# A fused retention and gated-MLP kernel whose engine order is a table: one table exchanged for another

## The chip, the cores and the metric

The kernel runs on one core of a Trainium2 chip. The metric is device time in microseconds (us), the median of three runs. One execution was also profiled by the hardware.

## The reference

A retention layer (a linear attention with a decaying state) feeds a gated MLP with a spatial gate. Everything is float32; B = 4, H = 8, S = 768, D = 64, model width 512.

```python
for t in range(S):                                   # retention, for each batch and head
    state = gamma * state + k[t] (x) v[t]
    y[t] = scale * q[t] @ state
x = y.transpose(0, 2, 1, 3).reshape(B, S, H * D)
h = gelu_tanh(x @ w_in)                              # moe: [B, S, 1024]
u, v = h[..., :512], h[..., 512:]
v_n = (v - mean(v)) / sqrt(var(v) + 1e-6) * g_ln
v_s = einsum('ts,bsd->btd', w_sg, v_n) + b_sg[None, :, None]
out = x + (u * v_s) @ w_out
```

## The kernel before

The work is cut into four batches b and two half sequences h of 384 positions; a pair of heads is p = 0..3. Each piece is a small function, and a table of words, `PROG`, calls them one after the other. A word is a letter and its indices, with D, G or A behind it where the piece may run on VectorE (DVE), GpSimd (POOL) or ScalarE (ACT): `I012D` is piece I of batch 0, half 1, pair 2, on VectorE. The schedule is manual: each engine works through its words in the order of the table and waits only for data and for buffers. So the table is the order of every engine and of the DMA issues of SyncE (SP).

The words that the change and the prediction speak of:

- L loads a pair's keys and values; `lo2`, `ls5` and the like load raw weights (of w_out and w_sg). All of these go through SP.
- P scales the keys (ACT or POOL), S and D are the score and state matmuls (TensorE, PE; tiles sc and ds), M masks the scores and T scans the states (DVE), W lays the scanned states beside the scores (ACT or POOL), O is the retention output (PE, tile po), X scales it into x (DVE), H and I split x into two float32r parts (cast and difference, tile xh).
- V and U are the two halves of the first MLP matmul (PE, tiles pv and pu), v and u their gelus (ACT), s the statistics (DVE), N the reciprocal deviation (six small operations of POOL, lines 378 to 383), n the normalisation (DVE, line 388), a and b its split (tile vh).
- G is the spatial matmul (PE, tile ps), e its scale and offset (DVE, line 435), m the gate, h and j the split of the product (tile gh), Y the last matmul (PE, tile py), r the residual and y the store.
- weights: r, k, c, b, a turn raw 64-bit words into float32, `hs7` and `os7` split part 7 of w_sg (lines 149 or 151, and 224).

All matmuls of the MLP are made of three float32r passes. PSUM has four banks for the retention (S, D and O share them) and four for the MLP, so a matmul that opens a bank waits for the reader of an earlier one: `S102` for `X100`, which reads `O100`, and `Y1000` for `e103`, which reads the last of four G banks.

Of the kernel before, what the change touches and what calls it, by code (L numbers as in the profile page):

```python
# [48 lines left out]
W0100A O003 bv1 ls2 W0101A av1 X003 H003A O010 lu3 I003D hv1A ls11 X010 U0001 hs0A ov1D ku2 H010A os0G V0011
ku1 L012 V0001 cu2 P011A cu1 V0012 ru2 bu2 ls9 ro3 V0002 bu1 ls1 ru1 V0013 I010G u000 V0003 v001 au2 V0021  # L50
s001 ru3 v000 S011 au1 hu2A s000 D011 ku3 M011 ou2G V0022 ko3 L013 hu1A T011 V0023 P012A ou1D S012 W0111A cu3
D012 co3 W0110A bu3 U0010 L100 v002 bo3 s002 au3 U0020 lo1 M012 lo0 U0011 P013A N00 ls7 hu3A T012 lo2 U0021
u001 W0120A ou3G O011 u002 S013 W0121A n000 n001 D013 a000 n002 O012 a001 b000D L101 ro1 b001D U0030 P100A
# [5 lines left out]
U0131 u012 n011 n012 O100 u013 n010 ho0G D102 a010 X100 a011 ao1 O101 T102 H100A D103 I100G a012 S102 ho1A
S103 b012D ho2A L110 X101 b010G W1021A G0020 M103 C111 L111 G0000 H101G M102 C110 b011G V1020 G0001 I101D oo0D  # L60
V1021 oo1G G0021 P110A oo2G G0002 ho3G G0022 e000 K102 m000D G0010 P111A oo3G h000 G0030 r000D G0011 j000G
G0031 W1020G T103 G0012 W1030A K103 G0032 W1031G e001 e002 V1010 m001G G0100 m002D h001 r001G h002 V1011 G0101
j002D j001D e003 r002G O102 D110 m003D O103 X102 h003 r003G T110 H102A D111 I102G S110 W1101A S111 j003D L112
M110 W1100G V1022 Y0000 T111 L113 C112 M111 G0102 W1110A W1111G C113 X103 Y0001 e010 H103G m010D G0110 I103D
y000 r010G P112A V1023 G0111 v102 s102 Y0020 G0120 P113A Y0021 G0121 y002 G0112 V1012 e011 Y0010 m011G V1013
r011D U1000 v101 s101 G0122 U1001 V1000 u100 Y0011 V1001 y001 G0130 V1002 G0131 V1003 G0132 v100 s100 Y0030
N10 U1010 h010 h011 Y0031 j010D n102 U1011 n100 n101 a100 j011D O110 a101 e012 b100G u101 D112 e013 a102 O111
X110 b101G T112 H110A D113 S112 y003 W1121A m013G S113 M112 L200 W1120G U1020 M113 m012G L201 Y0110 T113 h012
U1030 h013 j012G U1021 b102D I110D Y0100 j013D u102 X111 W1131G P200A V1100 r012D Y0111 H111G r013D U1031
I111G y011 V1120 W1130G P201A u103 V1101 V1121 Y0101 U1100 y010 V1110 O112 D200 X112 O113 H112A T200 D201  # L70
I112G S200 K200 X113 S201 W2001G M200 L202 H113A W2000G V1102 M201 V1122 I113G L203 V1111 T201 V1103 W2010A
W2011G V1123 v110 K201 V1112 v112 s110 Y0130 s112 P202A V1113 Y0131 v111 s111 Y0120 y013 N11 P203A U1110 Y0121
n110 n112 a110 U1111 n111 y012 b110G a111 U1120 a112 u111 b111D U1101 b112D U1121 u110 G1020 u112 G1000 G1021
U1130 G1022 G1030 U1131 G1031 u113 G1010 G1032 G1011 G1001 G1012 G1002 O200 e100 e101 D202 m100G X200 O201
H200A T202 m101G D203 h100 W2020A j100D S202 r100D h101 S203 e102 I200G L210 W2021A M202 G1100 r101G L211 X201
C210 G1120 K202 M203 H201A C211 G1101 m102D j101D h102 V2010 T203 r102G G1102 e103 W2031A j102G Y1000 W2030A
m103D e110 P210G G1121 h103 j103D Y1020 I201D r103D m110G Y1001 P211G Y1021 y100 K203 r110G Y1010 y102 V2011
Y1011 V2000 y101 G1122 V2001 V2020 O202 D210 X202 O203 H202A T210 D211 I202G S210 W2101A W2100G S211 X203 L212
M210 H203G V2012 C213 I203G M211 V2021 C212 L213 V2002 T211 V2013 W2111A V2022 W2110A V2003 V2023 v201 v200
s201 U2000 v202 s200 P212A U2010 s202 U2001 N20 U2011 u200 P213G Y1030 u201 n202 G1110 n201 h110 n200 j110G  # L80
Y1031 G1111 y103 G1130 G1112 a200 a201 b200D G1131 e111 b201G e112 U2020 a202 m112D U2030 m111G G1132 b202D
h111 h112 r111D U2031 j112G U2021 j111G e113 u203 m113G O210 u202 D212 r112G X210 h113 O211 H210A T212 j113G
D213 S212 W2121A I210D S213 W2120A r113D L300 M212 Y1130 T213 L301 Y1120 M213 W2130A W2131G Y1131 X211 Y1121
H211G y113 I211G V2100 y112 P300A Y1110 V2101 Y1111 V2120 P301A y111 V2110 V2121 V2111 Y1100 O212 D300 X212
O213 H212A T300 D301 I212G W3001A S300 K300 X213 W3000A S301 M300 L302 H213G V2122 I213G M301 V2102 L303 V2123
T301 V2103 v212 W3011G Y1101 W3010A s212 K301 v210 U2100 y110 s210 P302A U2110 V2112 U2111 V2113 P303A U2101
u211 v211 U2120 s211 u210 N21 U2130 U2121 n211 U2131 n210 u212 n212 a210 a211 O300 b210D a212 D302 b211G u213
X300 O301 H300A T302 b212G D303 W3021A S302 I300D S303 W3020G M302 L310 V3000 K302 X301 C310 G2030 L311 T303
H301A C311 G2010 I301D W3030A M303 K303 W3031G G2031 G2000 P310A G2032 G2001 G2011 P311A G2002 G2012 e200
m200G V3010 e201 V3001 m201D h200 r200G V3011 h201 G2020 j200D j201G O302 r201D D310 X302 O303 T310 H302A D311  # L90
I302G S310 W3101A W3100G S311 X303 L312 M310 H303A G2021 C313 I303G T311 C312 L313 V3012 M311 W3110A W3111G
G2022 V3013 e202 V3002 e203 m202G v301 Y2020 s301 m203G h202 Y2030 j202G h203 Y2000 j203D r202G Y2021 P313A
r203D Y2031 y202 P312G Y2001 y203 Y2010 y200 G2100 Y2011 G2120 y201 G2101 G2110 G2121 G2111 G2122 G2112 G2102
V3003 e210 e211 O310 v300 m210D D312 s300 m211G h210 O311 X310 r210G D313 h211 T312 S312 H310G W3121A S313
j210D I310D V3020 M313 W3120G G2130 r211G T313 V3021 X311 W3131A W3130G G2131 e212 H311A j211D V3022 M312
m212G G2132 I311G h212 V3023 e213 j212G Y2130 v302 r212D Y2120 s302 m213D Y2100 N30 h213 Y2110 j213D O312 n302
n300 O313 X312 r213G a300 Y2131 H312A b300D Y2101 n301 y213 I312G a301 Y2121 a302 y210 b301G X313 V3120 y212
Y2111 b302D H313G V3121 I313D y211 U3100 V3122 U3101 V3123 u310 V3100 v312 V3110 s312 V3101 V3111 V3102 V3112
V3103 V3113 v310 U3110 s310 v311 s311 U3120 N31 U3111 U3121 u311 n310 n312 U3130 a310 n311 u312 b310G a311
U3000 a312 U3131 b311D b312G U3010 u313 U3001 U3011 u300 G3000 u301 G3010 G3001 G3011 G3002 G3012 e300 m300G  # L100
U3020 e301 m301G h300 U3030 j300D h301 U3021 r300G U3031 u302 j301D r301G G3020 u303 G3030 G3021 G3031 G3022
G3032 e302 m302G e303 G3100 m303D h302 Y3020 r302D h303 j302D r303G G3101 j303D G3110 G3102 Y3021 e310 m310D
Y3030 y302 r310G G3130 G3111 G3131 G3112 G3132 e311 m311D Y3031 r311G G3120 y303 Y3010 G3121 Y3000 G3122 h310
# [482 lines left out]
```

## Time and profile before

| | |
|---|---|
| median of three runs | 410.04 us (409.76 to 411.33) |
| the profiled execution | 412.78 us, of which the span is 411.0 |
| TensorE | 398.8 us busy, 97% of the span |
| VectorE, GpSimd, ScalarE | 233.7, 180.6 and 145.4 us busy |

The span is what the profile shows, from the first instruction to the last. TensorE's busy time holds its warm-up matmuls (word `~40`, to 12 us) and matmuls that run at half clock, so it isn't all useful work.

### The profile page before, as it was taken

Reading aid. Unit: us, or ns where it says so; the run is one execution under the profiler, and the core shown is the slowest. Engines: PE = TensorE matmul, PEld = TensorE weight load, DVE = VectorE, ACT = ScalarE, POOL = GpSimd, SP = SyncE. Lnnn points to the kernel's source line nnn. Section 1 sums busy time; section 2 is a strip of 40 time slices with the busy share of each in tenths; the row PEclk is TensorE's granted clock in tenths of the full one; section 3 lists DMA queues with packets and bytes.
Section 4 is the critical chain, followed back from the end, with each engine's and each line's share of the span. In section 5 each row is a group of like instructions: output and inputs, shape, how many; then the busy total and the mean of one; then the engine's idle time right before and its main releaser. Section 6 shows DMA issues by size and latency. Waiting matters only on the chain.

```text
span 411.0 us, 9318 instructions
## 1 busy us (share of the span) xinstructions
PE 398.8 (97%) x3921; PEld 365.4 (89%) x3922; DVE 233.7 (57%) x373; ACT 145.4 (35%) x265; POOL 180.6 (44%) x217
## 2 busy tenths in 40 slices
...
GB/s 245 301 356 282 210 281 115 49 154 3 84 109 21 27 166 108 107 2 4 150 59 155 21 76 138 172 4 155 10 170 54 2 2 77 2 0 2 20 39 96
DMA packets 18122, 41.38 MB, mean 101 GB/s; under 512 B 2464, under 2 KB 8096, under 8 KB 18080
## 3 DMA queue, kind: packets, MB, share of 16 engines
...
q14 instruction: 11, 0.09, 0.1%
...
## 4 chain that ended last, share of the span: by engine, by line
PE 79%; DVE 9%; DMA 5%; issue 3%; POOL 1%; SPq 1%; ACT 1%; DVEq 0%
PE ps L425 24%; PE py L463 16%; PE pv L352 13%; PE pu L408 13%; PE po L320 5%; PE ds L271 4%; PE sc L279 4%; DMA raw<-in_w_u_dram 2%; DMA kt<-in_kk_dram 2%; DVE mw L297 2%; DVE sq L284 2%; DMA raw<-in_w_sg_dram 1%; DVE v L388 1%; DVE wx L188 1%; DVE ws L224 1%
## 5 line engine op out<-in xcount | busy, mean ns | idle before, releaser
L425 PE MATMUL ps<-ws,vh 128*128 128x384 f32 x576 | 107.8, 337 | 0.0
L425 PEld LDWEIGHTS ps<-ws,vh 128*128 128x128 f32 x576 | 101.5, 189 | 1.7
L352 PE MATMUL pv<-wv,xh 128*128 128x512 f32 x288 | 76.6, 400 | 1.4 <-ACT xh L149 1.3
L463 PE MATMUL py<-gh,wo 128*128 128x384 f32 x384 | 73.0, 336 | 1.1 <-DVE gt L435 1.1
L408 PE MATMUL pu<-xh,wu 128*128 128x384 f32 x384 | 73.0, 340 | 0.0
L463 PEld LDWEIGHTS py<-gh,wo 128*128 128x128 f32 x384 | 67.4, 188 | 2.9 <-issue 1.4
L408 PEld LDWEIGHTS pu<-xh,wu 128*128 128x128 f32 x384 | 67.4, 188 | 1.4 <-ACT v L362 0.2
L352 PEld LDWEIGHTS pv<-wv,xh 128*128 128x128 f32 x288 | 52.5, 188 | 12.4 <-ACT xh L149 2.1
L435 DVE SCALAR_TENSOR_TENSOR gt<-ps,gb 128x384 f32<-128x384 f32 x32 | 19.0, 611 | 57.9 <-PE ps L425 56.9
L446 POOL TENSOR_TENSOR gt<-gt,u 128x384 f32<-128x384 f32 x19 | 19.8, 1049 | 62.5 <-DVE gt L435 48.6
L149 ACT COPY mw<-sq 64x320 f32<-64x320 f32 (+1 forms) x41 | 33.8, 824 | 29.0 <-DVE sq L284 28.7
L297 DVE TENSOR_TENSOR mw<-sc,tab 64x384 f32<-64x384 f32 x64 | 35.5, 555 | 6.5 <-PE sc L279 4.9
L320 PEld LDWEIGHTS po<-mw 128*64 128x64 f32 (+1 forms) x768 | 26.6, 137 | 9.1 <-issue 5.0
L450 ACT CAST gh<-gt 128x384 fp32r<-128x384 f32 x32 | 16.2, 514 | 52.1 <-POOL gt L446 27.3
L320 PE MATMUL po<-mw 128*64 128x64 f32 (+1 forms) x768 | 31.6, 227 | 2.5 <-DVE sq L284 1.4
L339 POOL TENSOR_TENSOR xh<-x,xh 128x384 fp32r<-128x384 f32 x19 | 19.6, 1031 | 31.0 <-ACT xh L149 30.6
L284 DVE TENSOR_TENSOR_SCAN sq<-step,ds 128x384 f32<-128x384 f32 x32 | 30.2, 942 | 4.0 <-PE ds L271 2.1
L478 DVE TENSOR_TENSOR o<-py,o 128x384 f32<-128x384 f32 x32 | 17.6, 553 | 25.7 <-PE py L463 25.2
L366 DVE BATCH_NORM_STATS2 st<-v 128x6 f32<-128x512 f32 x24 | 16.4, 684 | 24.0 <-ACT v L362 23.9
L474 POOL TENSOR_TENSOR o<-xh 128x384 f32<-128x384 f32 x19 | 22.1, 1168 | 16.1 <-DVE gt L446 15.2
L362 ACT ACTIVATE v<-pv 128x512 f32<-128x512 f32 x24 | 14.3, 602 | 41.0 <-PE pv L352 40.9
L279 PE MATMUL sc<-mw,kt 64*64 64x64 f32 x768 | 26.9, 223 | 1.9 <-DVE x L327 1.8
...
## 6 DMA issues: line engine op xcount, KB each, us to landing
kt<-in_kk_dram SPq DMA_DIRECT2D x32, 384.0 KB, 5.2
...
```

Source lines behind the costliest of these rows:

```text
L149: nc.scalar.copy(out=out, in_=in_)
L279: mm(out=scs[u][o, c], lhsT=kt[i, c], rhs=mv[j][i, c], start=True, stop=True)
L284: nc.vector.tensor_tensor_scan(out=sqs[u].rearrange("p e c -> p (e c)"), data0=step_t[:, p].rearrange("p e c -> p (e c)"), data1=dss.pop(u ...
L297: nc.vector.tensor_tensor(out=mv[j][h], in0=sc[h], in1=mask_t[h, p : p + 1, :].to_broadcast([64, NCH, C]), op=ALU.mult,)
L320: mm(out=pos[u][o, c], lhsT=w[j][i, c], rhs=mv[j][i, c], start=True, stop=True)
L339: engines[e].tensor_tensor(out=t[:, p, 1], in0=xs.pop((b, hf, p)), in1=t[:, p, 0].bitcast(F32), op=ALU.subtract)
L352: mm(out=pv[b, hf, k], lhsT=x[:, p, a, k * 128 : (k + 1) * 128], rhs=wv_t[:, w, p], start=(p == 0 and n == 0), stop=(p == NP - 1 and n == 2),)
L408: mm(out=pu[b, hf, f], lhsT=wu_t[:, w, f, p * 128 : (p + 1) * 128], rhs=x[:, p, a], start=(n == 0), stop=(n == 11),)
L425: mm(out=ps[b, hf, d], lhsT=vh[b, t][:, v, d * 128 : (d + 1) * 128], rhs=ws_t[hf * NT + t][:, w], start=(n == 0), stop=(n == 3 * NT - 1),)
L446: engines[e].tensor_tensor(out=t, in0=t, in1=ut.pop((b, hf, d)), op=ALU.mult)
L463: mm(out=py[b, hf, c], lhsT=wo_t[c][:, w, d * 128 : (d + 1) * 128], rhs=gh[b, hf, d][:, a], start=(d == 0 and n == 0), stop=(d == 3 and n ...
L474: engines[e].tensor_tensor(out=o, in0=x[:, 0], in1=x[:, 1], op=ALU.add)
```

## The change

Only `PROG` is exchanged. The multiset of pieces is the same; 120 of the 1,224 words run on another engine, and many stand elsewhere. The counts of words on each engine stay about the same: DVE 316 before and 318 after, ACT 263 and 261, POOL 170 and 170, PE 416 and SP 89 in both. One line of the table and the line that stands at the same place after the change:

```diff
-hs9A os1D hs4A D100 os5D hs11A X013 hs2G D101 hs10A T100 H013A os9G S100 hs6A hs7A S101 I013D L102 hs8A os6D
+O013 hs1A D100 hs3G hs4A X013 D101 hs2G hs11A T100 H013A os9G S100 hs10A hs6A S101 I013D hs8A L102 os1D hs7A
```

The words of the diff are few to a reader; what follows are three places of the two orders, engine by engine.

VectorE in the first batch, from the splits of w_sg (`os`, line 224) to `X100` (line 327). Before, the rows from the last `os` over M (297), s (366 and 369), T (284), M and n (388) to X are:

```order
L224 TENSOR_TENSOR ws<-raw,ws 128x384
L297 TENSOR_TENSOR mw<-sc,tab 64x384 x2
L366 BN_STATS st<-v 128x6
L369 BN_AGGR mvar<-st 128x2
L284 SCALAR_TENSOR_TENSOR sq<-step,ds 128x384
L366 BN_STATS st<-v 128x6
L369 BN_AGGR mvar<-st 128x2
L366 BN_STATS st<-v 128x6
L369 BN_AGGR mvar<-st 128x2
L297 TENSOR_TENSOR mw<-sc,tab 64x384 x2
L388 TENSOR_SCALAR v<-v,mvar,lny 128x512 x3
L327 TENSOR_TENSOR x<-po,tab 128x384
```

and after the change:

```order
L224 TENSOR_TENSOR ws<-raw,ws 128x384 x6
L297 TENSOR_TENSOR mw<-sc,tab 64x384 x2
L366 BN_STATS st<-v 128x6
L369 BN_AGGR mvar<-st 128x2
L366 BN_STATS st<-v 128x6
L369 BN_AGGR mvar<-st 128x2
L366 BN_STATS st<-v 128x6
L369 BN_AGGR mvar<-st 128x2
L284 SCALAR_TENSOR_TENSOR sq<-step,ds 128x384
L297 TENSOR_TENSOR mw<-sc,tab 64x384 x2
L388 TENSOR_SCALAR v<-v,mvar,lny 128x512 x3
L327 TENSOR_TENSOR x<-po,tab 128x384
```

The scan `T101` moved behind the three statistics, and with it M behind it is `M100`, which both `O100` on PE needs. In front, six `os` stand in a row (`os1 os3 os6 os2 os4 os8`); before there were four there and one weight operation (`bo1`, line 188), and two others further up. POOL has `os7 os10 os11 ao1` beside them after the change, and had `os3 os2 os7` and, later, `os11` before; `ao1` stood behind N.

ScalarE in the same batch, from the split of x for pair 1 (`H011`, tile xh) to the W that `O013` needs (tile mw). Before:

```order
L149 CAST xh<-x 128x384
L394 CAST vh<-v 128x512
L178 ACTIVATE wx<-raw 128x512
L418 ACTIVATE u<-pu 128x384
L178 ACTIVATE wx<-raw 128x512
L149 CAST xh<-x 128x384
L197 ACTIVATE raw<-raw 128x512
L178 ACTIVATE wx<-raw 128x512
L256 ACTIVATE kt<-kt,tab 128x384
L149 COPY mw<-sq 64x64x6
```

and after:

```order
L149 CAST xh<-x 128x384
L197 ACTIVATE raw<-raw 128x512
L394 CAST vh<-v 128x512
L197 ACTIVATE raw<-raw 128x512
L149 CAST ws<-raw 128x384
L149 CAST xh<-x 128x384
L418 ACTIVATE u<-pu 128x384
L178 ACTIVATE wx<-raw 128x512 x2
L149 COPY mw<-sq 64x64x6
L256 ACTIVATE kt<-kt,tab 128x384
L149 COPY mw<-sq 64x64x6
```

Between the two `xh` rows (`H011` and `H012`) stood `a002 ko2 u003 ko0` (lines 394, 178, 418, 178); now `ro1 a002 ro0 hs5` (197, 394, 197 and 149, ws) stand there, and `ko2 ro2` went ahead of the first. Of the two W of `O013`, one came over from POOL. On SP, the loads of w_out come in the order `lo2 lo1 lo0` with `ls5 ls11` behind them, where it was `lo1 lo0 ls7 lo2`.

VectorE in the second batch, at the change from the G of half 0 to those of half 1. Before, from `j100` to `e103` (lines 454 and 435):

```order
L454 TENSOR_TENSOR gh<-gt,gh 128x384
L474 TENSOR_TENSOR o<-xh 128x384
L435 SCALAR_TENSOR_TENSOR gt<-ps,gb 128x384
L297 TENSOR_TENSOR mw<-sc,tab 64x384 x2
L327 TENSOR_TENSOR x<-po,tab 128x384
L297 TENSOR_TENSOR mw<-sc,tab 64x384 x2
L446 TENSOR_TENSOR gt<-gt,u 128x384
L454 TENSOR_TENSOR gh<-gt,gh 128x384
L284 SCALAR_TENSOR_TENSOR sq<-step,ds 128x384
L435 SCALAR_TENSOR_TENSOR gt<-ps,gb 128x384
```

and after:

```order
L454 TENSOR_TENSOR gh<-gt,gh 128x384
L435 SCALAR_TENSOR_TENSOR gt<-ps,gb 128x384
L297 TENSOR_TENSOR mw<-sc,tab 64x384 x2
L284 SCALAR_TENSOR_TENSOR sq<-step,ds 128x384
L297 TENSOR_TENSOR mw<-sc,tab 64x384 x2
L435 SCALAR_TENSOR_TENSOR gt<-ps,gb 128x384
```

Between `j100` and `e103` VectorE has eight pieces before and four after (an M is one piece of two instructions); `j101`, one of the eight, went to POOL. On PE, `O202 D210 O203 D211 S210 S211` now stand between the last G of half 0 and the first of half 1, and `G1100 G1120` alone between those and `Y1000`; before, `G1100 G1120 G1101 V2010 G1102` stood there.

## Rows read from the trace of the kernel before

**Rows 1.** The page's first line: the span of the profiled execution.

```profile
span 411.0 us, 9318 instructions
```

**Rows 2.** Windows: length, each engine's busy time (instructions), granted clock, DMA share, GB/s.

```profile
32.00:34.00 2.00, 1.18 (x35) 1.04 (x33) 1.23 (x2) 1.88 (x3) 1.20 (x1) 1.00 1.06 296
...
84.00:86.00 2.00, 2.00 (x48) 1.96 (x42) 1.19 (x2) 2.00 (x5) 1.12 (x2) 0.57 0.04 12
...
204.00:404.00 200.00, 200.00 (x1802) 189.73 (x1802) 100.07 (x162) 53.96 (x98) 78.21 (x96) 1.00 0.20 60
```

**Rows 3.** Timeline of TensorE: start, length, instruction, [idle before <-who ended it].

```profile
78.17 1.22 PE L320 MATMUL po<-mw 64*64 64x64 f32 x24
...
81.02 0.92 PE L271 MATMUL ds<-mw,kt 64*64 64x64 f32 x24
83.74 2.41 PE L279 MATMUL sc<-mw,kt 64*64 64x64 f32 x48 [1.81 <-DVE x L327]
86.08 3.08 PE L425 MATMUL ps<-ws,vh 128*128 128x384 f32 x12
89.00 0.85 PE L352 MATMUL pv<-wv,xh 128*128 128x512 f32 x3
```

**Rows 4.** The chain that ended last: the same matmuls elsewhere (start, length).

```profile
107.84 1.40 PE sc L279 x48
...
119.17 2.08 PE ps L425 x12
```

**Rows 5.** Timeline of VectorE, 67 to 84 us.

```profile
67.54 3.24 DVE L224 TENSOR_TENSOR ws<-raw,ws 128x384 fp32r<-128x384 f32 x3
70.71 1.50 DVE L188 SCALAR_TENSOR_TENSOR wx<-raw,wx 128x512 int32<-128x512 int32 x1
72.13 0.55 DVE L224 TENSOR_TENSOR ws<-raw,ws 128x384 fp32r<-128x384 f32 x1
...
74.58 0.93 DVE L284 TENSOR_TENSOR_SCAN sq<-step,ds 128x384 f32<-128x384 f32 x1
...
76.93 0.18 DVE L369 BATCH_NORM_AGGREGATE mvar<-st 128x2 f32<-128x6 f32 x1
77.14 1.14 DVE L297 TENSOR_TENSOR mw<-sc,tab 64x384 f32<-64x384 f32 x2
79.56 3.67 DVE L388 TENSOR_SCALAR v<-v,mvar,lny 128x512 f32<-128x512 f32 x3 [1.27 <-POOL lny L383]
83.14 0.54 DVE L327 TENSOR_TENSOR x<-po,tab 128x384 f32<-128x384 f32 x1
```

**Rows 6.** Timeline of GpSimd, 67 to 80 us.

```profile
67.75 3.91 POOL L224 TENSOR_TENSOR ws<-raw,ws 128x384 fp32r<-128x384 f32 x3
...
77.20 0.24 POOL L378 TENSOR_SCALAR lna<-mvar 128x3 f32<-128x3 f32 x1 [0.34 <-DVE mvar L369]
...
79.33 0.19 POOL L383 TENSOR_TENSOR lny<-lny,lnt 128x3 f32<-128x3 f32 x1
```

**Rows 7.** Timeline of TensorE, 56 to 64 us.

```profile
56.51 3.90 PE L352 MATMUL pv<-wv,xh 128*128 128x512 f32 x15 [0.67 <-ACT xh L149]
61.08 2.49 PE L352 MATMUL pv<-wv,xh 128*128 128x512 f32 x9 [0.67 <-ACT xh L149]
63.49 1.05 PE L320 MATMUL po<-mw 128*64 128x64 f32 x24
```

**Rows 8.** Timeline of ScalarE, 59 to 63 us.

```profile
59.02 0.67 ACT L178 ACTIVATE wx<-raw 128x512 f32<-128x512 f32 x1 [2.05 <-DMA raw<-in_w_out_dram]
...
62.69 0.89 ACT L149 COPY mw<-sq 64x384 f32<-64x384 f32 x1
```

**Rows 9.** Timelines of TensorE and VectorE near 200 us.

```profile
200.97 1.28 PE L463 MATMUL py<-gh,wo 128*128 128x384 f32 x6 [1.12 <-DVE gt L435]
...
200.24 0.58 DVE L435 SCALAR_TENSOR_TENSOR gt<-ps,gb 128x384 f32<-128x384 f32 x1
```

**Rows 10.** DMA issues of the page: size, median time from issue to landing.

```profile
kt<-in_kk_dram SPq DMA_DIRECT2D x32, 384.0 KB, 5.2
```

More of the change, by code (lines that the diff above doesn't have):

```diff
@@ L49 @@
[L49 to L53, printed above, removed]
@@ L54 @@
-X011 ao3 ro0 Q M013 V0120 ls5 H011A ls3 U0031 a002 I011D T013 b002G ko2 V0121 u003 X012 V0110 ko0 co2 V0100
-W0130G H012A ro2 V0111 I012D ko1 co0 V0101 P101A bo2 V0122 W0131A bo0 V0112 co1 hs5A ao2 V0102 hs1A hs3A O013
-hs9A os1D hs4A D100 os5D hs11A X013 hs2G D101 hs10A T100 H013A os9G S100 hs6A hs7A S101 I013D L102 hs8A os6D
-W1000A U0100 os4D os10D L103 V0123 bo1 os8D U0101 v012 M101 K100 W1001A os3G V0113 u010 s012 V0103 os2G v011
-T101 U0110 v010 os7G s011 P102A U0120 W1011A K101 s010 os11G W1010A U0111 M100 N01 U0130 u011 P103A U0121 ao0
@@ L59 @@
[L59 to L103, printed above, removed]
@@ new lines @@
+O003 bv1 ls9 W0101A ls6 av1 X003 lu3 H003A O010 I003D hv1A L012 X010 U0001 hs0A ov1D ku2 P011A os0D V0011 cu2
+ku1 V0001 H010G ls8 ru2 bu2 V0012 ls3 ru1 I010D V0002 ro3 cu1 au2 u000 V0013 V0003 v001 bu1 V0021 hu2A s001
+au1 v000 S011 ru3 s000 D011 ku3 ou2G M011 ko3 V0022 L013 P012A T011 hu1G S012 D012 ls2 ou1D W0111A cu3 V0023
+L100 W0110A co3 bu3 U0010 v002 bo3 lo2 U0020 s002 au3 lo1 lo0 M012 U0011 N00 P013A ls5 T012 hu3A ls11 U0021
+u001 W0120A ou3G O011 u002 S013 W0121A n000 D013 n001 a000 n002 O012 a001 L101 b000D P100A U0030 b001D ko2
@@ new lines @@
+X011 ao3 Q ro2 V0120 M013 ls7 H011A V0110 ro1 I011D U0031 a002 co2 ls1 X012 ro0 b002G T013 V0121 hs5A H012A
+V0111 os5D u003 V0100 ko0 I012D bo2 ko1 V0122 co0 W0130A V0101 co1 bo0 P101A V0112 bo1 W0131A V0102 ao2 hs9A
+O013 hs1A D100 hs3G hs4A X013 D101 hs2G hs11A T100 H013A os9G S100 hs10A hs6A S101 I013D hs8A L102 os1D hs7A
+U0100 W1000A os3D os6D L103 V0123 os2D os4D U0101 v012 os8D W1001A M101 K100 V0113 os7G u010 V0103 s012 v011
+os10G U0110 v010 s011 P102A os11G U0120 s010 ao1 T101 U0130 M100 W1011A U0121 N01 W1010A U0131 P103A K101 u012
@@ new lines @@
+n011 U0111 u013 n012 n010 O100 ao0 u011 a010 D102 a011 X100 b010G O101 a012 T102 H100A D103 ho0A b012D S102
+W1020A I100G S103 ho1A M102 L110 b011G ho2A G0020 ho3A X101 L111 M103 C111 G0000 H101A oo1G C110 W1021A V1020
+I101D G0001 oo2G V1021 oo0D G0002 P110A oo3G G0021 e000 K102 m000G T103 G0010 W1030A K103 G0022 r000D h000
+P111G W1031A G0011 j000G G0030 G0012 G0031 e001 e002 m001G V1010 G0032 m002D h001 r001D h002 V1011 j001D r002D
+G0100 e003 j002G Y0000 m003D r003D h003 G0101 j003D Y0001 G0102 y000 G0110 e010 m010D G0120 r010G G0111 G0121
@@ new lines @@
+X200 b112G T202 H200A D203 I200G S202 S203 W2020G X201 L210 M202 H201A G1020 K202 C210 W2021G L211 M203 C211
+G1000 I201G T203 G1021 W2031A K203 G1030 W2030A G1022 P210A G1031 G1010 G1032 P211G G1011 G1001 G1012 G1002
+O202 e100 e101 D210 m100G X202 O203 T210 m101G h100 D211 S210 W2100A j100D W2101G S211 e102 h101 L212 M210
+m102G G1100 T211 C213 L213 j101G h102 G1120 M211 W2111A j102G Y1000 W2110A e103 r100G G1101 C212 r101D Y1020
+m103G G1121 P212G h103 j103G G1102 r102G Y1001 e110 P213A r103D Y1021 m110D y100 H202G Y1010 r110G y102 V2000
@@ new lines @@
+I202D Y1011 X203 H203G V2001 I203G y101 V2010 V2020 V2011 V2021 V2012 G1122 V2013 V2022 v201 V2002 s201 V2023
+V2003 v202 Y1030 s202 v200 s200 U2000 h110 j110G U2010 N20 U2001 U2011 u200 n202 n201 Y1031 u201 n200 G1110
+y103 G1130 G1111 a200 a201 b200D G1131 b201D U2020 a202 b202G G1132 U2021 G1112 u202 U2030 e111 e112 O210
+m111D m112G h111 D212 X210 O211 r111D H210A D213 h112 T212 j111G S212 W2121A j112D S213 e113 r112G L300 W2120A
+M212 Y1130 m113G L301 T213 Y1120 h113 r113G M213 W2131A Y1110 j113G U2031 I210D W2130G X211 Y1131 u203 P300A
@@ new lines @@
+Y1121 H211A y113 I211D Y1111 y112 V2120 y111 P301A V2100 V2121 V2101 V2110 Y1100 V2111 Y1101 O212 y110 D300
+X212 O213 H212A T300 D301 I212D W3000A S300 K300 X213 W3001G S301 H213A M300 L302 I213G V2122 M301 V2102 L303
+V2123 T301 V2103 v212 W3011G V2112 s212 v210 W3010G U2100 s210 K301 U2110 P302A V2113 U2111 v211 s211 U2101
+u211 P303A N21 U2120 u210 U2130 n210 n211 a210 U2121 n212 a211 b210D a212 U2131 b211D u212 b212G O300 u213
+D302 X300 O301 H300A T302 D303 I300D W3020A S302 W3021G X301 S303 M302 L310 H301G K302 V3000 C310 I301G T303
@@ new lines @@
+C311 G2010 L311 M303 W3030A K303 G2000 W3031A G2030 G2001 P310G G2031 G2002 G2032 e200 m200G G2020 P311G h200
+G2011 j200G G2021 r200G G2012 G2022 e201 m201D V3010 e202 h201 V3001 r201D j201D V3011 m202G e203 Y2020 m203D
+h202 Y2030 r202G h203 j202D O302 r203D D310 j203G X302 O303 H302A T310 D311 I302D S310 W3100A W3101G X303 S311
+M310 L312 H303A I303G Y2021 C313 T311 C312 L313 Y2031 M311 W3111A W3110G V3012 y203 V3002 y202 Y2000 V3013
+P312A G2120 v301 s301 Y2001 Y2010 y200 P313A G2110 Y2011 G2111 y201 G2100 G2112 G2121 G2101 G2122 G2102 V3003
@@ new lines @@
+e210 e211 O310 v300 m210D D312 s300 m211G h210 O311 X310 r210G D313 h211 T312 H310A S312 j211G W3120A S313
+M312 I310G V3020 M313 G2130 W3121G e212 r211G V3021 T313 G2131 m212G X311 W3131A V3022 j210D h212 r212D G2132
+j212D W3130G V3023 e213 H311G Y2130 v302 m213D s302 h213 r213G Y2120 I311D Y2100 N30 Y2110 j213D O312 n302
+O313 n300 X312 a300 n301 Y2131 H312A b300G a301 Y2121 a302 y213 I312G V3120 y212 b301G Y2101 X313 H313A V3121
+I313D y210 b302G V3100 V3122 U3100 V3123 V3101 v312 U3101 s312 V3102 u310 V3110 V3103 V3111 v310 Y2111 s310
```

27 lines of the change are left out of this document (21 added, 6 removed).

## The prediction

> **What bounds the kernel now.** I read the windows first, then TensorE's timeline, then the engines it waits for. The long window from 204 to 404 us shows TensorE busy for 200.00 of 200.00 us at a granted clock of 1.00 [rows 2]: there it is the bound, and an order can only lose. What an order can win are the places where TensorE stands still or runs slowly, and the timeline of the first 90 us holds nearly all of them.
>
> The dearest place is `S102`. After the states end at 81.02 + 0.92 = 81.94, TensorE waits 1.81 us for `X100` [rows 3]. Then it is slow: the 48 score matmuls take from 83.74 to 86.08, 2.34 us, and the first 12 spatial matmuls from 86.08 to 89.00, 2.92 us [rows 3]; elsewhere the same work takes 1.40 and 2.08 us [rows 4]. The window from 84 to 86 us tells why: the granted clock is 0.57 there, near the lower of the two levels, 1.2 and 2.4 GHz [rows 2]. So the place costs 1.81 + 0.94 + 0.84 = 3.6 us.
>
> The second is smaller: two waits of 0.67 us for the split of x (`H011` and `H012`), at 56.51 and 61.08 [rows 7]. The third is a wait of 1.12 us of `Y1000` for `e103`, at 200.97 [rows 9], the one large wait that I found behind 90 us. In the first 36 us there are more, but as far as `O010` and `U0001` the new table keeps the order of TensorE and of those VectorE pieces (scans, masks, x) for which it waits, so I leave them as they are.
>
> **Part A, up to O013 (the ScalarE rows of the change).** `H011` now comes before `ro1` and `ro0`, and its two predecessors need the load that now lands first, so both waits of 0.67 us should shrink. But what comes behind them has to be ready too, and `O013` needs both its W. Before, ScalarE waits 2.05 us for the third w_out load until 59.02, then runs seven operations, and starts the last W at 62.69 [rows 8]; it takes 0.89 us, and TensorE starts `O013` at 63.49 [rows 7], with its first matmuls behind that W's end. After, `hs5` needs `ls5`, which stands behind the same three w_out loads: these four transfers (three of w_out, one of w_sg) are of the same bytes as the four that had landed by 59.02, only in another order. From there ScalarE again has seven operations to run before the last W (`hs5 H012 u003 ko0 ko1 W0130 P101`). So the W starts at about 62.7 again, and what TensorE gains at `H011` it waits at `O013`. I take 0. The bounds: 1.34 us gained, if the loads land that much earlier, and 0.9 us lost, the length of the W that came to ScalarE's queue from POOL [rows 8].
>
> **Part B, S102 (the VectorE rows of the change).** `X100` stands behind three normalisations, which wait for N, which waits for the last statistic. Before, that statistic ends at 76.93 + 0.18 = 77.11 [rows 5], N runs on POOL from 77.20 to 79.52 [rows 6], the three normalisations take 3.67 us, and X starts at 83.14 [rows 5].
> After, the scan of 0.93 us no longer stands before the statistics, but more `os` do. How long do these take? Before, VectorE's three beside POOL's took 3.24 us and the weight operation next to them 1.50, but the one alone 0.55 [rows 5]; POOL's three took 3.91, 1.30 each [rows 6]. So beside POOL, VectorE gets about one through per operation of POOL. After, VectorE is free for its six at about 66.9: `O013` ends near 64.5 [rows 7], and `X013`, `D100`, the scan and `I013` follow it (0.54, 0.92 and 0.93 us are the rows for the first three [rows 3, 5]). One runs alone (0.55), four beside the four of POOL (4 x 1.30 = 5.2), the last alone (0.55): until 73.2. Then M (1.14) and three statistics (0.80 each: before, two lie between the scan's end at 75.51 and 77.11 [rows 5]) end at 76.8, hardly earlier than before.
> N then ends near 79.2. Two things differ. First, `M100` now stands behind the scan: 76.8 + 0.93 + 1.14 = 78.9, where it ended at 77.14 + 1.14 = 78.28 [rows 5]. `O100` stands at 78.17 [rows 3] and needs both halves, so TensorE waits about 0.7 there. Second, POOL has `ao1` behind it already, so one of the two long operations beside the normalisations is gone: I take 3.0 us for them in place of 3.67 (three at 0.55 are the lower bound). `X100` then ends at 79.2 + 3.0 + 0.54 = 82.75, against a TensorE that arrives at 81.94 + 0.7 = 82.65. A wait of 0.1, and I add 0.2 for the splits of x that follow: the place costs 0.7 + 0.3 where it cost 3.6. **Part B: -2.6 us.** Bounds: if no operation is held up, nothing waits (-3.6); if the normalisations still take 3.67, `X100` is 0.7 later (-1.9).
> This rests on the clock staying up. Between 32 and 34 us TensorE is busy for only 1.18 of 2 us, and the granted clock is 1.00 [rows 2]; so I take it that waits of 0.7 and 0.1 us, 4 us apart, leave it up. The Trainium skill says it otherwise ("TensorE: Matmul & The Clock Gate", section "What's actually happening"): the gate goes by how busy the engine has been recently, so no single wait decides. By the page alone, several shorter waits could bring the clock down as the one of 1.81 did; this is the rival "clock" below.
>
> **Part C, Y1000.** Before, `e103` starts at 200.24 behind eight pieces that follow `j100` [rows 9]; after, four stand there, and six retention pieces of TensorE lie between the G whose banks are to be emptied and the matmul that needs the bank. I take 0.2 us of the 1.12 as left: **-0.9 us** (bounds: all gone, -1.12; nothing gained, 0).
>
> **Part D, new waits.** TensorE has no slack behind 90 us, and 120 pieces change engine there and before. Eleven splits j go from VectorE to POOL and six back, eight residuals r from POOL to VectorE and four back; each stands in a chain e, m, h, j to a Y. On POOL, `P111` now stands ahead of `j000` and waits for a load that takes 5.2 us from its issue [rows 10]; the issue follows `S103`, which comes earlier now, and several us of TensorE's work lie between, so that costs nothing while TensorE is on time, and up to one operation of POOL (1.30) if not. I can't find a place where a chain is surely too long, but several where its cover is a few tenths (`Y0001`, `Y1001`, `G2110`). The old table left one wait of 1.12 us behind 90 us [rows 9]. I take **+0.7 us**, with bounds of 0 and 2.2, two such waits.
>
> On SP the order of the loads changes, and nothing but A and `P111` stands close behind a load. The tail from the last Y to the last store has the same pieces: 0.
>
> **Sum.** 0 - 2.6 - 0.9 + 0.7 = -2.8 us. The profiled execution took 412.78 us with a span of 411.0 [rows 1], so this gives 410.0 for it. It is 2.74 us over the median of 410.04; all terms are waits within the span, so I take them off the median as well: **407.2 us**.
>
> **The rivals.**
> "Clock" (page and mechanism above): the two waits of B bring the clock down. Then 0.94 + 0.84 = 1.78 us stay, and the sum is -1.0: 409.0 us. For it: B leaves two waits within 5 us. Against it: the window at 32 to 34 us.
> "Waits elsewhere": B and C come out as said, but the chains of part D lose 2.2 us or more, and A its 0.9: 0 - 2.6 - 0.9 + 2.2 + 0.9 = -0.4, 409.6 us. For it: seventeen j and twelve r on other engines. Against: nearly all of TensorE's long busy windows.
> "VectorE late" (slower): all six `os` take the 1.50 us of the longest operation there [rows 5]. Then they end at 66.9 + 9.0 = 75.9, M and the statistics at 79.4, `M100` at 81.5. `O100` waits 3.3 us, N ends at 81.8, X at 81.8 + 3.67 + 0.54 = 86.0, against a TensorE at 81.94 + 3.3 = 85.2; it waits 0.8 more, and the clock falls as before (1.78): 5.9 us in place of 3.6. With C and D that is +2.1: 412.1 us. It decides from where the last statistic ends after 79.4; up to 77.3 there is still a gain. Against it: POOL has only four operations to hold VectorE up.
> "Free VectorE": nothing holds VectorE up, -3.6 at B, -1.12 at C, 0.3 at D and half of A's bound: 404.9 us.
>
> **How the numbers follow.** My forecast has 0.5, and its own range, from the bounds of B and C, is 406.0 to 408.5. "Clock" has 0.15, "waits elsewhere" 0.12, "VectorE late" 0.09 and "free VectorE" 0.14. The range of 8 in 10 reaches from the fast case to past "waits elsewhere": 404.9 to 410.8; it leaves out "VectorE late" and the ends. About 0.5% is what a measurement of this kernel can tell from no change, 2.05 us: under 408.0 or over 412.1. Faster: 0.14 and 0.42 of the forecast's 0.5, 0.56. Slower: most of "VectorE late" and a little of the rest, 0.10. The same: 0.34.
>
> **What would show it.** Right: no window between 82 and 90 us below a clock of 0.9; `S102` starts within 0.5 us of the states before it; `O100` waits for VectorE (line 297); `Y1000` waits for nothing; `O013` starts within 0.5 us of 63.5. Wrong: a wait over 1 us at `S102`, a half-clock window anywhere, `O013` a microsecond later, or waits of TensorE behind 90 us of more than 2 us in sum.

## The result and the profile after

The changed kernel takes 408.73 us (median of 20 executions, 407.74 to 411.15), the kernel before 411.89 (20 executions beside them, 409.76 to 414.66): a ratio of 0.9934, with a 95% interval of 0.9915 to 0.9952, or 3.2 us. The profiled execution took 411.15 us, the longest of the 20. TensorE's mean granted clock, which each execution reports, says why: 18 of the 20 have 0.998 or more and a median of 408.72; the profiled one and one other have 0.996, and their median is 411.09.

So the comparison must be made with the clock in view. The clocks of those 20 executions of the kernel before were not kept; beside the experiments below it was executed 103 more times, 43 times with a mean clock of 0.998 or more (here called full clock; median 410.21), 60 times below (412.65). Full clock against full clock the change is worth 410.21 - 408.72 = 1.5 us; the other 1.7 us of the 3.2 go with how often the clock falls: in 60 of 103 executions before, in 2 of 20 after. The split is rough: the 103 fall into four groups, whose medians at full clock go from 409.94 to 411.00, and by means in place of medians the two parts are 1.8 and 1.1 us.

The first line of the page of after, against [rows 1]:

```profile
span 409.4 us, 9339 instructions
```

Windows of the same profile, with the columns of [rows 2] and against them:

```profile
32.00:34.00 2.00, 1.06 (x24) 0.89 (x24) 1.68 (x4) 1.74 (x2) 0.62 (x1) 1.00 1.00 322
34.00:36.00 2.00, 1.77 (x25) 1.68 (x26) 0.83 (x3) 1.82 (x5) 0.68 (x1) 0.55 1.06 418
36.00:38.00 2.00, 2.00 (x8) 1.95 (x8) 2.00 (x4) 2.00 (x5) 0.90 (x1) 0.59 1.06 303
...
84.00:86.00 2.00, 2.00 (x29) 1.93 (x24) 1.94 (x4) 2.00 (x5) 1.82 (x3) 1.00 0.40 115
```

The stretch near half clock behind `S102` is gone (84 to 86 us: 1.00). In this execution there is one from 34 to 38 us instead, where before's profile had full clock:

```profile
34.00:36.00 2.00, 2.00 (x28) 1.64 (x23) 1.81 (x4) 1.93 (x5) 0.85 (x2) 1.00 1.03 294
```

The two waits of TensorE ahead of it are nearly the same in the two profiles, before

```profile
31.77 1.06 PE L320 MATMUL po<-mw 64*64 64x64 f32 x24 [0.95 <-DVE sq L284]
33.66 0.92 PE L320 MATMUL po<-mw 128*64 128x64 f32 x24 [0.82 <-DVE x L327]
```

and after:

```profile
32.35 1.06 PE L320 MATMUL po<-mw 64*64 64x64 f32 x24 [0.94 <-DVE sq L284]
34.23 1.55 PE L320 MATMUL po<-mw 128*64 128x64 f32 x24 [0.82 <-DVE x L327]
```

TensorE's timeline of the profile after, from `O100` to the first spatial matmuls, against [rows 3]:

```profile
78.94 0.29 PE L320 MATMUL po<-mw 64*64 64x64 f32 x2 [0.39 <-DVE mw L297]
79.43 1.06 PE L320 MATMUL po<-mw 64*64 64x64 f32 x22 [0.20 <-DVE mw L297]
...
82.11 0.91 PE L271 MATMUL ds<-mw,kt 64*64 64x64 f32 x24
82.86 1.69 PE L279 MATMUL sc<-mw,kt 64*64 64x64 f32 x48
84.48 2.37 PE L425 MATMUL ps<-ws,vh 128*128 128x384 f32 x12
86.68 0.85 PE L352 MATMUL pv<-wv,xh 128*128 128x512 f32 x3
```

`S102` follows the states without a wait; the wait that is left, 0.39 + 0.20 us, is that of `O100` for `M100`. VectorE's timeline of the same stretch, against [rows 5]:

```profile
67.20 6.58 DVE L224 TENSOR_TENSOR ws<-raw,ws 128x384 fp32r<-128x384 f32 x6
...
77.18 0.18 DVE L369 BATCH_NORM_AGGREGATE mvar<-st 128x2 f32<-128x6 f32 x1
77.28 0.92 DVE L284 TENSOR_TENSOR_SCAN sq<-step,ds 128x384 f32<-128x384 f32 x1
78.23 1.14 DVE L297 TENSOR_TENSOR mw<-sc,tab 64x384 f32<-64x384 f32 x2
79.81 2.44 DVE L388 TENSOR_SCALAR v<-v,mvar,lny 128x512 f32<-128x512 f32 x3 [0.44 <-POOL lny L383]
82.17 0.55 DVE L327 TENSOR_TENSOR x<-po,tab 128x384 f32<-128x384 f32 x1
```

The statistics end at 77.36, in front of the scan, as late as before; the normalisations behind N take 2.44 us where they took 3.67. Behind 90 us, TensorE's waits in the profile after (us in total, times, longest) are two, and `Y1000`'s 1.12 us [rows 9] is none of them:

```profile
PE py L463 <- DVE gt L435: 0.5, 1, 0.5
PE pu L408 <- ACT u L418: 0.3, 1, 0.3
```

They stand at `Y0000` (101.67 us) and `U1030` (about 141 us).

### The profile page after: what moved, and what is told of

Read it like the earlier page. It is cut to its first block, busy times and chain, and to the rows that moved or that the text cites. A ratio compares the mean times of both kernels' runs of the same rounds, so it can differ in the third digit from the quotient of the medians.

```text
span 409.4 us, 9339 instructions
## 1 busy us (share of the span) xinstructions
PE 399.9 (98%) x3922; PEld 366.1 (89%) x3922; DVE 225.8 (55%) x375; ACT 144.2 (35%) x263; POOL 183.6 (45%) x217
## 4 chain that ended last, share of the span: by engine, by line
PE 79%; DVE 8%; DMA 8%; ACT 2%; issue 2%; POOL 1%; SPq 1%; DVEq 0%
PE ps L425 24%; PE py L463 16%; PE pv L352 12%; PE pu L408 12%; PE po L320 6%; PE ds L271 5%; PE sc L279 4%; DMA raw<-in_w_u_dram 2%; DMA raw<-in_w_out_dram 2%; DMA kt<-in_kk_dram 2%; DMA raw<-in_w_sg_dram 2%; DVE ws L224 1%; DVE mw L297 1%; DVE sq L284 1%; DVE st L366 1%
## 5 line engine op out<-in xcount | busy, mean ns | idle before, releaser
L425 PE MATMUL ps<-ws,vh 128*128 128x384 f32 x576 | 105.9, 336 | 0.0
L408 PE MATMUL pu<-xh,wu 128*128 128x384 f32 x384 | 74.1, 343 | 0.4 <-ACT u L418 0.3
L408 PEld LDWEIGHTS pu<-xh,wu 128*128 128x128 f32 x384 | 68.6, 190 | 2.6 <-ACT u L418 0.7
L149 ACT COPY mw<-sq 64x320 f32<-64x320 f32 (+1 forms) x42 | 34.8, 828 | 35.6 <-DVE sq L284 35.2
L446 POOL TENSOR_TENSOR gt<-gt,u 128x384 f32<-128x384 f32 x20 | 21.5, 1078 | 57.3 <-DVE gt L435 57.1
L362 ACT ACTIVATE v<-pv 128x512 f32<-128x512 f32 x24 | 14.4, 599 | 50.5 <-PE pv L352 50.0
L454 POOL TENSOR_TENSOR gh<-gt,gh 128x384 fp32r<-128x384 f32 x17 | 18.0, 1062 | 25.0 <-ACT gh L450 25.0
L151 POOL COPY mw<-sq 64x320 f32<-64x320 f32 (+1 forms) x22 | 21.6, 981 | 15.3 <-DVE sq L284 8.8
L271 PE MATMUL ds<-mw,kt 64*64 64x64 f32 x704 | 27.0, 222 | 0.3 <-ACT wu L149 0.2
```

The costliest lines, as they stand in the source:

```text
L149: nc.scalar.copy(out=out, in_=in_)
L151: engines[e].tensor_copy(out=out, in_=in_)
L271: mm(out=dss[u][o, :, c + hf], lhsT=ks[i, c], rhs=w[j][i, c], start=True, stop=True)
L408: mm(out=pu[b, hf, f], lhsT=wu_t[:, w, f, p * 128 : (p + 1) * 128], rhs=x[:, p, a], start=(n == 0), stop=(n == 11),)
L425: mm(out=ps[b, hf, d], lhsT=vh[b, t][:, v, d * 128 : (d + 1) * 128], rhs=ws_t[hf * NT + t][:, w], start=(n == 0), stop=(n == 3 * NT - 1),)
L446: engines[e].tensor_tensor(out=t, in0=t, in1=ut.pop((b, hf, d)), op=ALU.mult)
```

## The experiments

In their profiles the lines of the code count one higher, since the table is a line longer. The clock is told as the number of executions at full clock, that is with a mean granted clock of 0.998 or more. Ratios and their intervals are against executions of the kernel before that ran beside the experiment; a difference of two experiments' medians is less sure than either ratio.

**1 and 2. The two halves of the table.** `G0020`, just behind `S102`, is the cut: one kernel has the changed order up to it and the old one behind it, the other the reverse.

```diff
 (table of the kernel after, first word to G0020)
+(table of the kernel before, its words that are not yet placed, in their order)
```

> The table of after up to G0020, the table of before from there on. Theory 'place' (most of the gain lies where S102 waited, the rest at Y1000): S102 waits for nothing, no half-clock window near 84 us, and the 1.12 us wait at Y1000 stays; 2 to 3 us under before, ratio about 0.994. Rival 'spread' (the gain is made by many small things in the 300 us behind the head): within 1 us of before, ratio over 0.9975.

> The table of before up to G0020, the table of after from there on. 'Place': S102 still waits about 1.8 us and the clock falls behind it; only Y1000's wait changes, 0.5 to 1 us under before, ratio 0.9975 to 0.999. 'Spread': 2 us or more under before, ratio under 0.995.

Measured: with the head changed, 408.96 us (ratio 0.9939, 0.991 to 0.9968; 11 of 12 at full clock, median of these 408.83); in its profile the clock is 1.00 from 28 us to the end, `S102` waits for nothing, and `Y1000`'s wait of 1.1 us stays. With the rest changed, 413.12 (1.0046, 1.0016 to 1.0076; 3 of 12 at full clock). The whole gain is the head's: the full change has 408.72 at full clock, 0.1 less than the head alone. The rest behind the old head is slower by 1.0 us, which neither theory had. Its profile shows the old wait of `S102`, none at `Y1000`, and two waits that the old order didn't have there:

```profile
85.54 1.78 PE L280 MATMUL sc<-mw,kt 64*64 64x64 f32 x48 [1.81 <-DVE x L328]
...
92.36 0.50 PE L353 MATMUL pv<-wv,xh 128*128 128x512 f32 x1 [0.55 <-DVE xh L340]
...
105.23 0.93 PE L464 MATMUL py<-gh,wo 128*128 128x384 f32 x4 [0.49 <-DVE gt L436]
```

With one of 0.3 us at `U1030` the new waits are 1.4 us in sum, against the 1.12 that went, so they account for 0.3 us of the 1.0; the rest stays open. And in this execution the clock did not fall behind the wait of 1.81 us, but from 34 to 38 us, as in the profile of the changed kernel:

```profile
34.00:36.00 2.00, 1.85 (x25) 1.77 (x26) 0.83 (x2) 1.90 (x4) 0.85 (x2) 0.51 0.99 307
36.00:38.00 2.00, 2.00 (x8) 1.95 (x8) 2.00 (x3) 1.91 (x5) 1.83 (x2) 0.63 0.95 327
...
86.00:88.00 2.00, 2.00 (x44) 1.85 (x41) 1.19 (x2) 2.00 (x5) 1.32 (x2) 1.00 0.12 25
```

Where the clock fell in executions that were not profiled, their mean clock doesn't tell.

**3 and 4. The place of the scan, alone.** In the kernel before, `T101` and what follows from it go behind the statistics; in the second kernel POOL's `ao1` also goes ahead of N.

```diff
-v011 T101 U0110 v010 os7G s011 P102A U0120 W1011A K101 s010 os11G W1010A U0111 M100 N01
+v011 U0110 v010 os7G s011 P102A U0120 os11G s010 T101 W1011A W1010A U0111 M100 N01 K101
```

> Before, with the scan T101 (0.93 us) put behind the three statistics, and on POOL os11 and N ahead of the carry copy that waits for T101. 'Place': N starts 0.9 us earlier, X100 ends 0.9 earlier, S102 waits about 0.9 us in place of 1.8; if the half clock came from that one wait, it is gone too: 1 to 2.7 us under before. 'Spread': under 0.5 us.

> The same, and ao1 ahead of N on POOL, so that one POOL operation less runs beside the three normalisations (3.67 us before, about 2.9 then). 'Place': X100 ends some 1.6 us earlier than before, S102 waits 0.2 us or less, no half clock, and M100 is as early as before, so O100 doesn't wait: 3 to 3.6 us under before, more than after gains at this place. 'Spread': under 0.5 us.

Measured: 410.24 us (0.9968, 0.9941 to 0.9995; 9 of 12 at full clock) and 410.19 (0.9958, 0.993 to 0.9986; 10 of 12). Both profiles show `S102` with no wait and `O100` idle for 0.6 us for `M100`, as after the change; in the first:

```profile
78.70 0.29 PE L321 MATMUL po<-mw 64*64 64x64 f32 x2 [0.42 <-DVE mw L298]
79.19 1.06 PE L321 MATMUL po<-mw 64*64 64x64 f32 x22 [0.20 <-DVE mw L298]
...
82.81 1.78 PE L280 MATMUL sc<-mw,kt 64*64 64x64 f32 x48
```

So moving one scan takes the wait of 1.81 us away at the price of 0.6, and the clock stays up more often; moving `ao1` adds nothing that these runs can show. That `S102` would still wait for 0.9 us in the first kernel, and that `O100` would not wait and 3 us be won in the second, fell: `M100` stands behind the scan in both.

**5. The scan put back in the changed kernel.**

```diff
-v010 s011 P102A os11G U0120 s010 ao1 T101 U0130 M100
+v010 T101 s011 P102A os11G U0120 s010 ao1 U0130 M100
```

> The changed kernel with the scan T101 put back ahead of the statistics; all else as changed. Theory 'scan' (the place of the scan is what freed S102): the last statistic, N and X100 each come 0.93 us later, M100 no longer stands behind the scan, so O100 waits about 0.9 us less, and S102 waits about 0.8 us; the time is 0 to 0.9 us longer than that of the changed kernel, and some more executions show a stretch at half clock. Rival 'ao1 and the splits' (S102 is free because one long GpSimd operation is gone from beside the normalisations and the splits stand further ahead): the order of the scan makes no difference, S102 waits under 0.3 us and the time is that of the changed kernel within 0.3 us.

Measured: 410.00 us (0.995, 0.9925 to 0.9975; 11 of 12 at full clock, 409.8), 1.1 to 1.3 above the changed kernel by medians and 0.7 by the two ratios, whose intervals overlap. Its TensorE timeline has a wait at `S102` again, and those at `O100` remain (0.36 and 0.20 us), since `M100` is late with or without the scan in front of it:

```profile
82.80 1.77 PE L280 MATMUL sc<-mw,kt 64*64 64x64 f32 x48 [0.59 <-DVE x L328]
```

The theory of the scan holds for the wait, which the rival had under 0.3 us; the part of it that had `O100`'s wait vanish fell. A wait of 0.59 us here hardly ever brought the clock down.

**6. The chain in front of `O100`.** One of the six splits goes behind `M100`.

```diff
-W1000A os3D os6D L103
+W1000A os3D L103
...
-M100 W1011A
+M100 os6D W1011A
```

> The changed kernel with one split of w_sg, os6, moved from the row ahead of the statistics to behind M100 on VectorE. Theory 'chain' (O100 waits for the chain splits, M, statistics, scan, M100): the chain is shorter by one split, 0.55 to 1.3 us, O100's two waits of 0.9 us in sum shrink to 0.3 or less, S102 still waits for nothing, and the time falls by 0.4 to 0.9 us. Rival 'retention queue' (VectorE's next piece is late by the moved split, and TensorE waits there instead): O100's waits shrink but S102 waits for X100, which now stands behind the split, by as much, and the time stays within 0.3 us.

Measured: 408.54 us (0.9928, 0.9895 to 0.996; 8 of 8 at full clock). In the profile the waits of `O100` for `M100` are gone and `S102` waits for nothing. In VectorE's timeline the five splits took 4.17 us where six took 6.58, and the sixth stands behind `M100`:

```profile
64.64 4.17 DVE L225 TENSOR_TENSOR ws<-raw,ws 128x384 fp32r<-128x384 f32 x5
...
74.33 0.55 DVE L225 TENSOR_TENSOR ws<-raw,ws 128x384 fp32r<-128x384 f32 x1
75.25 2.44 DVE L389 TENSOR_SCALAR v<-v,mvar,lny 128x512 f32<-128x512 f32 x3 [0.37 <-POOL lny L384]
```

The moved split takes 0.55 us in the time in which VectorE waits for N anyway. The waits behaved as the chain theory said; the median fell by only 0.2 us, and eight executions spread over 3 us can't tell 0.2 from 0.7.

**7. Head and rest mended.** The head of after with the rest of before, `os6` as in 6, and `r100` behind `e103`.

```diff
-j100D S202 r100D h101
+j100D S202 h101
...
-e103 W2031A j102G Y1000
+e103 r100D W2031A j102G Y1000
```

> The changed order up to G0020, the order before from there on, with two mends: os6 behind M100 and the residual r100 behind e103. Theory 'places' (the head's gain and the waits behind it are independent, each worth its own length): O100's waits fall from 0.9 to 0.3 or less, Y1000's wait of 1.1 us falls by the 0.55 us of one piece or more, and the time is 0.9 to 1.7 us under that of the same kernel without the mends (408.96): 407.3 to 408.1. Rival 'given back' (what one wait gives up the next one takes, since TensorE's pieces behind it then come earlier than their inputs): within 0.4 us of 408.96.

Measured: 406.66 us (0.9882, 0.9843 to 0.9921; 5 of 6 at full clock), 2.3 under the same kernel without the mends, more than expected. Behind 90 us its profile shows no wait of TensorE at all. Counted from the first score matmul, its last store is 2.9 us earlier than in kernel 1's profile; the lead is 0.9 at `O100`, 1.5 at `V1021`, which stands behind `S102`, and 3.0 at `Y1000`.

**8. Part A alone.** In the kernel before: the loads of w_out in the order `lo2 lo1 lo0 ls7`, and ScalarE's words so (with `W0130` on ScalarE, `b002` behind `a002`); `hs5` and its load stay where they were, so this is the changed order without that one operation:

```diff
-ro1 P100A ro0 H011A a002 ko2 u003 ko0 H012A ro2 ko1
+P100A ko2 ro2 H011A ro1 a002 ro0 H012A u003 ko0 ko1 W0130A
```

> The kernel before with the changed order of ScalarE and of the w_out loads alone around H011 and H012 (part A of the prediction). The prediction's step (what is gained at H011 and H012 is waited for at O013): the two waits of 0.67 us shrink by 0.5 us or more in sum, O013 starts within 0.3 us of its time before, counted from the first score matmul, and the time is within 0.5 us of the kernel before. Rival 'A gains' (W0131 comes early enough as well): O013 starts 0.6 to 1.3 us earlier and S102 waits longer by as much for X100, which VectorE sets, so that the time still changes by less than 0.5 us, while the wait of S102 grows to 2.3 to 3.1 us.

Measured: 412.29 us (1.0008, 0.9983 to 1.0033; 4 of 12 at full clock). In the profile the waits of `H011` and `H012` are down to 0.27 us, and `O013` and its two W come early. The two W on ScalarE's timeline:

```profile
60.03 0.92 ACT L150 COPY mw<-sq 64x384 f32<-64x384 f32 x1
...
61.36 0.89 ACT L150 COPY mw<-sq 64x384 f32<-64x384 f32 x1
```

and on TensorE, `O013` and `S102`:

```profile
62.16 1.05 PE L321 MATMUL po<-mw 128*64 128x64 f32 x24
...
82.43 1.83 PE L280 MATMUL sc<-mw,kt 64*64 64x64 f32 x48 [1.81 <-DVE x L328]
```

Counted from the first score matmul (12.03 here, 12.17 before), `O013` starts 1.2 us earlier than before, and `S102` too, with the same wait of 1.81: VectorE's chain to `X100` starts from `O013` and moves with it. That is neither theory. And yet the median is that of before; run 10 looks into it.

**9. The wait filled.** Six matmuls that nothing reads go ahead of `S102` in the kernel before. They only make TensorE work while it waits; they leave no work out.

```diff
+    def fill(n):
+        t = psm.tile([128, DF], F32, tag="m", name="wp")
+        for _ in range(n):
+            mm(out=t, lhsT=wv_t[:, 0, 0, :128], rhs=wv_t[:, 0, 0], start=True, stop=True)
...
-D103 I100G a012 S102
+D103 I100G a012 F6 S102
```

> The kernel before with six more matmuls of TensorE (128x512, on weights, into a bank that nothing reads) ahead of S102, so that TensorE works where it stood still for 1.81 us. X100 comes no earlier, so S102 can't start earlier: all that can change is the clock. Theory 'standing still' (the half clock behind S102 follows from the wait there): the profiled execution shows a granted clock of 0.9 or more from 82 to 90 us, the share of executions with a mean clock of 0.998 or more rises from 25 of 60 to over three quarters, and the median falls by 0.8 to 1.8 us. Rival 'weak work' (the small 64x64 matmuls ahead of and behind the wait bring the clock down, wait or not): the share stays below a half and the time within 0.6 us of before.

> The kernel before with the six filling matmuls ahead of S102 once more, as the neighbour of the run with part A: 410.0 to 411.0 by either theory, as in its first run (410.56).

Measured: 410.56 us (0.9966, 0.9937 to 0.9996) and, again, 410.65 (0.9988, 0.9955 to 1.0021); 10 of 12 executions at full clock each time, where the kernel before has 43 of 103. TensorE's timeline in the first of the two profiles (L499 is the filling):

```profile
80.63 1.66 PE L499 MATMUL wp<-wv 128*128 128x512 f32 x6
82.52 1.77 PE L280 MATMUL sc<-mw,kt 64*64 64x64 f32 x48 [0.23 <-DVE x L328]
84.23 2.38 PE L426 MATMUL ps<-ws,vh 128*128 128x384 f32 x12
```

and its window behind the wait:

```profile
84.00:86.00 2.00, 2.00 (x21) 1.93 (x17) 1.83 (x3) 1.95 (x5) 2.00 (x2) 1.00 0.50 168
```

`X100` comes no earlier and the score matmuls start no earlier; only the clock differs. The full-clock executions take 410.48, those of before 410.21. So most of the falls in before come from TensorE's standing still at `S102` (60 of 103 executions, against 4 of 24 with the wait filled), not from the small matmuls around it.

**10. Part A with the wait filled**, so that the clock doesn't cover it.

> Part A alone in the kernel before, as in an earlier run, and with the six filling matmuls ahead of S102, so that the clock's fall there doesn't cover what part A is worth. Theory 'A gains' (the changed order of ScalarE and of the w_out loads makes TensorE wait less at H011, H012 and O013; the traces so far show 0.3 to 2.2 us of waits there in the order before, 0 to 1.1 in the changed one): 0.6 to 1.2 us under the filled kernel without part A that runs beside it. Rival 'A is nothing' (the prediction's 0: what TensorE gains there it gives back at S102): within 0.4 us of it, with the two filling matmuls' stretch followed by a longer wait for X100.

Measured: 410.43 us (0.9977, 0.9951 to 1.0003; 12 of 12 at full clock) beside 410.65 for the filled kernel without A: 0.2 less, which these runs can't tell from nothing, and a narrower spread (409.5 to 411.2 against 409.1 to 413.6). The two profiles of the filled kernel say what A does. They have the same order, and ScalarE's wait for the third w_out load is 1.40 us in one and 2.54 in the other. The first, on ScalarE's timeline:

```profile
57.77 0.68 ACT L179 ACTIVATE wx<-raw 128x512 f32<-128x512 f32 x1 [1.40 <-DMA raw<-in_w_out_dram]
```

and the second, of the run made again:

```profile
59.24 0.66 ACT L179 ACTIVATE wx<-raw 128x512 f32<-128x512 f32 x1 [2.54 <-DMA raw<-in_w_out_dram]
```

In the first TensorE lost 0.3 us at `H011` and `H012`, in the second 0.8 + 0.3. What the old order costs here hangs on when a load lands in that execution; the 1.34 us of [rows 7] are one draw. What profiled executions show for A (about 1 us) is more than the 0 to 0.2 of the medians, and why stays open.

**11. The new waits mended.** The changed kernel with `os6` as in 6, `r001` behind `e003`, and `u102` ahead of `a101`.

```diff
-h001 r001D h002
+h001 h002
...
-e003 j002G Y0000
+e003 r001D j002G Y0000
...
-a101 U1011 u102 b100D
+u102 a101 U1011 b100D
```

> The changed kernel with three places mended: os6 behind M100 (as in the run above), the residual r001 behind e003 on VectorE (ahead of Y0000, which waits 0.49 us), and the gelu u102 ahead of the split a101 on ScalarE (ahead of U1030, which waits 0.34 us). Theory 'each wait its length' (part D's new waits behind 90 us cost what they show): Y0000 and U1030 wait for nothing, and the time is 0.7 to 1.2 us under that of the same kernel with os6 alone moved (408.54): 407.3 to 407.8. Rival 'given back' (TensorE's later pieces then wait for what still comes at the same time): the two waits go, others of the same sum appear behind them, and the time stays within 0.4 us of 408.54.

Measured: 407.33 us (0.9901, 0.9867 to 0.9935; 7 of 9 at full clock), 1.2 under kernel 6. The profile shows no wait of TensorE behind 90 us; `Y0000` follows its predecessor at once:

```profile
97.24 1.20 PE L464 MATMUL py<-gh,wo 128*128 128x384 f32 x6
```

From the first score matmul to the last store it takes 390.53 us, kernel 6 391.71, and kernel 7 390.54: two orders of the rest, both without waits, end within 0.01 us of each other in their profiles. The medians of kernels 7 and 11 are both under the changed kernel's 408.73; their intervals overlap each other and that of the changed kernel (0.9915 to 0.9952), so that they are faster rests on the waits that are gone from their profiles.

## Why the prediction came out as it did

The forecast was 407.2 us with 404.9 to 410.8, from -2.8; measured were 408.73 and -3.2. Faster by more than 0.5% was the likeliest case, and it came. 408.73 lies inside the range and just outside the forecast's own range of 406.0 to 408.5, whose upper end, by the bounds of B (-1.9) and C (0) with D's +0.7, should have read 408.8. The absolute time is 1.5 us off mostly because the reference of 410.04 was a median of three executions, where 20 gave 411.89.

- **The clock (-1.78 of part B).** The result is right, the step that argued it is not. "Between 32 and 34 us ... so I take it that waits of 0.7 and 0.1 us leave it up" took one execution's window for a property of the program. The profile after has the same two waits there (0.94 and 0.82 us, ending at 32.35 and 34.23) and the clock behind them is 0.55; the sign named for "wrong", a half-clock window anywhere, was seen. Whether the clock falls differs from execution to execution of one kernel, with odds that change with the waits: with the wait of 1.81 us at `S102`, full clock in 43 of 103 (before), 3 of 12 (kernel 2) and 4 of 12 (kernel 8); without it, or with it filled, in 111 of 127 (the changed kernel and the other ten kernels, of which run 5 has a wait of 0.59 there). The cause is shown by run 9, which fills TensorE's wait and leaves the rest of the order as it was: 20 of 24 at full clock. The Trainium skill ("TensorE: Matmul & The Clock Gate", section "What's actually happening") says that the gate looks at recent activity over spans that run freely of the kernel, so that the same kernel can differ from run to run; the odds above agree with that. The rival "clock", which had the two waits of B bring it down as the one did, fell: 2 of 20.
- **The size of the clock's part.** A fall goes with 2.4 us by before's two medians, more than the 1.78 of the stretch, which was itself too high: the 48 and 12 matmuls behind `S102` take 1.62 and 2.20 us at full clock in the profile after (82.86 to 84.48 to 86.68), not the 1.40 and 2.08 of [rows 4], so the stretch cost 1.44. That the clock's part came out at 1.1 to 1.7 us, near 1.78, is luck in part: the one profile that was read is of the 60 kind, and with one of the 43 the term would not have been there.
- **The waits of part B.** Each step came out near: the last statistic ended at 77.36 (76.8 forecast), `M100` at 79.37 (78.9), `O100` waited for 0.39 + 0.20 us and ended at 80.49, 0.9 later than if its 1.06 us had followed the U before it at once (77.33 + 1.22 + 1.06 = 79.61; 0.7 forecast), N ended at 79.78 (79.2), the normalisations took 2.44 (3.0), `X100` ended at 82.72 (82.75), and `S102` waited for nothing (0.1). The six splits were sized at 6.3 us and took 6.58. Experiments 3 and 5 show that the scan's place does it, the latter at 0.7 to 1.3 us.
- **Part A (0).** `O013` started at 63.93, within 0.5 us of 63.5 as named, but in an execution with a stretch near half clock at 34 to 38 ahead of it. The last W started at 62.98, near the 62.7 of the step "so the W starts at about 62.7 again", but that step doesn't hold in general. In run 8, without `hs5`, the last W starts at 61.36, since ScalarE waits for 0.23 us only for its last w_out load; and the wait of 2.05 us in the old order, on which the step stood, is 1.40 to 2.76 us in six profiles of that order. Counted from the first score matmul, the last W starts between 48.9 and 50.5 us in the six profiles of the whole new head and between 49.4 and 51.8 in these six (50.5 in the one that the prediction read). In time, A is worth 0 to 0.2 (runs 8 and 10), so the term was sized rightly for a reason that didn't hold.
- **Part C (-0.9) and D (+0.7).** `Y1000` waits for nothing, so C was 1.1. Part D's new waits were two, 0.49 and 0.34; mending them gave 1.2 us. None stood at the places named (`Y0001`, `Y1001`, `G2110`). Together they were to be -0.2; by these waits they are -0.3, and full change against head alone is -0.1. Behind the old head the same rest cost 1.0 us (run 2), so C and D have no worth that can be told apart from the head's, and why isn't shown.
- **The sum at full clock.** Waits: -0.9 (B), 0 to -0.2 (A) and -0.1 to -0.3 (C and D) make -1.0 to -1.4, where the medians give -1.5. What is missing is not assigned; medians at full clock scatter by more (409.94 to 411.00 for the kernel before).
- **"Waits elsewhere" and "VectorE late"** fell: waits behind 90 us are 0.8 in sum, and the last statistic came before 77.4, where "VectorE late" needed 79.4.
